# Sparse attention and a softplus layer on one core: another written-out order for the five engines

## The chip, the core and the metric

The kernel runs on one core of a Trainium2 chip. A core has five engines, each with an instruction queue of its own that it works off in order: TensorE (PE in the profile; PEld are its weight loads), VectorE (DVE), ScalarE (ACT), GpSimd (POOL) and SyncE (SP, which here only issues DMAs). Engines wait for one another through semaphores. The metric is the device time in microseconds (us).

## What is computed

For 4 batches of 8 heads, 768 positions and a head size of 64: keys are cut into chunks of 32; for each query the chunks are ranked by an upper bound of its scores (from each chunk's least and greatest key), and a causal softmax attention runs over the best six. Its output goes through a layer of 512 to 2048 to 512 with a softplus.

```python
k_min = np.min(k_chunks, axis=3)
k_max = np.max(k_chunks, axis=3)
ub = np.sum(np.maximum(q[:, :, :, None, :] * k_min[:, :, None, :, :], q[:, :, :, None, :] * k_max[:, :, None, :, :]), axis=-1)
...
top_chunks = np.argsort(ub, axis=-1)[..., -top_k:]
...
scores = np.where(mask, scores, -1000000000.0)
...
h = x @ w_in
g = np.maximum(h, 0.0) + np.log1p(np.exp(-np.abs(h)))
return (g @ w_out).astype(np.float32)
```

## The kernel before

The work is cut into 12 blocks of 256 queries, n = 0 to 11; three of them (k = n mod 3) make one batch. A block's heads are taken as four pairs. Every step of every block is an operation of a plan, made in `make_plan`; its name carries the block, as in kx3. These are the steps, in the order of a block's life:

- ld k, q, v (L378): loads from HBM with a cast to bf16, two for each tensor of a block, issued on GpSimd. Block 0's keys and queries come by SP and are cast on chip (cast).
- kD, qD (L499): transposition of keys and queries by a DMA, issued on SP, from block 3 on. Blocks 0 to 2 use TensorE instead (kT, qT, L495), with a copy (qc).
- kx, kn (L514, L522): greatest and least key of each chunk, on VectorE. bd (L298, into `bd`): these laid out as a block-diagonal operand. kc: the keys copied to their places (`ka`, `kb`).
- qpn (L571 on ScalarE, L573 and L575 on VectorE): positive and negative part of the queries. qac: the queries' copy for the other head of a pair.
- ub (L594): the chunk bounds, on TensorE; uba (L606), mx (L617, L621), raw (L636, L639): causal mask, the six greatest, and a raw 0/1 mask in `mraw`, on VectorE.
- mD (L660): the raw mask transposed by a DMA that SP issues (mT on TensorE before block 3). mc: the mask copied into spare rows of the query operand, so that the scores come out masked.
- s (L711, L712): scores on TensorE, into PSUM. ex (L719): exp on ScalarE. af (L729): the causal triangle set to zero on GpSimd. av (L741): products with the values. nm (L751, L752): division by the row sum, on VectorE.
- xD (L756): the result transposed by DMA, or oT (L767) on TensorE and a copy xc, for blocks 0, 1, 2 and 11.
- h (L910): product with w_in. e, ln (L915, L920): exp and ln(1 + e) on ScalarE, into `g`.
- y: product with w_out. Blocks 0, 1 and 11 do it plainly (L940). Blocks 2 to 10 use a scheme with seven products in place of eight (`seven`, L855), which needs differences of g (dl, dh, dd, de, df, L838) and combines the results (yr, yz, yv, yc, yd, ye, yw, yx, yf, L870). st (L952, L891): the store of 128 rows of output, issued on SP.
- ws, wd, wh, wv: for the seven products, rows of w_out are loaded once more (ws, L809, on SP, into the four `ysb` buffers that also hold outputs) and sums and differences of them are made (L815, on GpSimd or VectorE): wd and wh one half each (128 x 256), wv over the whole width (128 x 512). There are 8 wd, 16 wh and 8 wv. The first y of block 2 needs all the wv, its second product all the wh.

What stands where is not found at run time. A table, `ORDER` (L201 to L284), lists every operation once, and `in_order` reads it; an engine executes its operations in the table's order:

```python
for word in table.split():
    if word[0] == "z":
        order.append(int(word[1:]))
        continue
    name, _, which = word[1:].partition("#")
```

The letter in front of a name is the engine: P TensorE, A ScalarE, V VectorE, G GpSimd, S SP. A name stands for its next operation that has not been placed, or with # for a certain one. zN is N matrix products of zeros on TensorE, with no use but to keep it busy (L1025). Buffers and PSUM banks are given out in the table's order too, so an operation may also wait for the last reader of the buffer that it gets. Loads of the weights and of block 3 have fixed waits of their own (`gate`): block 3's loads wait for the last chunk of w_out.

Each engine's queue is strict: on GpSimd a load that stands behind an af waits until that af's exp is done; on SP a transposition that stands behind a ws waits until the buffer of this ws is free.

Of the kernel before, what the change touches and what calls it, by code (L numbers as in the profile page):

```python
# [213 lines left out]
Ps1 Ps2 Aex1 Ph0#5 Aex2 Gaf1 Gw_out2 PoT1 Pav1 Ae0#5 Pav1 Ps2#5 Ae0 Ps2#6 Vnm1 Gw_out3 Sws1.1 Sws1.0 Sws0.1 Sws0.0
Ph0 Aex2#5 Aex2#6 Gaf1 PoT1 Ps2#8 Gld_k4.0 Aln0 Pav1 Vxc1#2 Pav1 Vxc1 Ps2 Vnm1 Ph0 Gld_k4.1 Aex2 Aex2#8 PoT1 Ps2#3
Gld_k5.0 Ae0 Vxc1 Py0 Aex2#3 Gld_k5.1 Ps2 Ae0 Ps2 Vwh1 Ph1 Aex2 Vwv1 Gwh1 Aex2 Ps2#11 Gaf2#1 Ph0 Ae1 Gaf2 Aex2#11
Gld_q4.0 Pav2 Aln0 Pav2 Ps2#10 Gld_q4.1 Vnm2 Ps2 Ae0 Ph1 Vwd0 Aex2#10 Gaf2 Vwd1 Aln0 PoT2 Gaf2 Py0 Vwv0 Aex2 Ps2 Py0
Aex2 Ae1 Pav2 Ps2 Aln1 Pav2 Ps2#14 Ph1#4 Vnm2 Gld_k3.0 Aln0 Vwh0#1 Ph1 Gld_k3.1 Aex2 PoT2 Aex2#14 Ps2#16 SkD4
Gld_q3.0 Ae1 Py0 Axc2 Vxc2 Aex2#16 Ps2#18 Vye0 Sws2.0 Ae1#4 Ps2#20 Ph1 Aex2#18 Sws2.1 Aex2#20 Ph1#6 Ae1 Gaf2#6
Ps2#17 SqD4 Py0 Aex2#17 Aln1 Gaf2#5 Ps2#23 Ps2#15 Gld_q3.1 Py0 Aex2#15 Vkx4 SkD3 Aex2#23 Gld_q5.0 Ps2#19 Ph1#7  # L220
Aex2#19 Vkn4 Sohk Gld_q5.1 Ae1#6 Py0 Ae1#7 Gwh0 Vkc4 Ps2#22 Aln1#3 Ph1 Gwd2 Vwh2#1 Vbd4 Gaf2 Aex2#22 Ps2 Py0 Vkc4
Gaf2 Aex2 Gld_v3.0 Vqac4 Ps2 Aye0 Pav2 Gld_k6.0 Pav2 SqD3 Ae1 Py1 Vnm2 Aex2 Gwv2 Vkx3 PoT2 Pav2 Axc2 Pav2 Aln1 Gwh2
Py1 Sws3.0 Vnm2 Vkn3 Sohk PoT2 Py1 Axc2 Sws3.1 Ph2 Sst0 Vkc3 Aqpn3 SkD5 Vbd3 Ph2 Vqpn3 Ae2 Gwh3 Vqac3 Skb0 Pub3 Ae2
Gld_q10.0 Ph2 Vuba3 Vmx3 Ph2 Gld_v4.0 Vraw3 Py1 Gwv3 Sws4.1 Vqpn4 Aqpn4 Ae2 Aln2 Vwd3 Pub4 Ae2 Vkx5 Gwh3 Ph2#7
Sws4.0 Aln2 Gld_k6.1 SmD3 Vuba4 Ph2#6 Aye1 Vmx4 Gld_k9.0 Py1 Ae2#6 Gld_k9.1 Ae2#7 Ph2 Vraw4 Aln2#3 Gwh4#1 Vkn5 Ph2
# [834 lines left out]
```

## Time and profile before

| | us |
|---|---|
| median of 3 runs | 271.03 |
| lowest, highest | 269.88, 272.91 |
| profiled execution, its own time | 271.5 |
| its span, first to last instruction | 269.8 |
| TensorE busy | 254.3 |
| ScalarE busy | 220.6 |
| VectorE busy | 193.7 |
| GpSimd busy | 136.6 |
| mean granted TensorE clock | 0.987 of full |

All times in what follows count from the start of the span. The profile's row for a group of instructions gives its busy time, the mean of one in ns, the engine's idle time just before and what ended it. A row of the chain of waits gives start, length and what the end of the kernel was waiting for then; a row of the stretches gives, for a stretch of time, each engine's busy time with its count, then the granted clock, the DMA engines and GB/s.

### The profile page before, as it was taken

Reading aid. Unit: us, or ns where it says so; the run is one execution under the profiler, and the core shown is the slowest. Engines: PE = TensorE matmul, PEld = TensorE weight load, DVE = VectorE, ACT = ScalarE, POOL = GpSimd, SP = SyncE. Lnnn points to the kernel's source line nnn. Section 1 sums busy time; section 2 is a strip of 40 time slices with the busy share of each in tenths; the row PEclk is TensorE's granted clock in tenths of the full one; section 3 lists DMA queues with packets and bytes.
Section 4 is the critical chain, followed back from the end, with each engine's and each line's share of the span. In section 5 each row is a group of like instructions: output and inputs, shape, how many; then the busy total and the mean of one; then the engine's idle time right before and its main releaser. Section 6 shows DMA issues by size and latency. Waiting matters only on the chain.

```text
span 269.8 us, 7644 instructions
## 1 busy us (share of the span) xinstructions
PE 254.3 (94%) x2987; PEld 218.1 (81%) x2995; DVE 193.7 (72%) x589; ACT 220.6 (82%) x396; POOL 136.6 (51%) x220
## 2 busy tenths in 40 slices
PE   8899999995898779999999999999999999999995
PEld 7889898673575558889988899889899998899873
DVE  6788935449998998997989789887865526647310
ACT  3989899994587967899989999798989999756671
POOL 8986579467775967877675392330610411200000
PEclk9999999999799979999999999999999999999999
DMA  8999999999999999999999499654143040004004
GB/s 171 126 141 213 242 201 195 150 175 198 275 125 188 171 213 195 85 108 99 144 157 132 118 109 180 133 45 86 22 100 79 12 143 6 2 0 158 4 0 157
DMA packets 117028, 34.12 MB, mean 126 GB/s; under 512 B 104800, under 2 KB 111968, under 8 KB 116992
## 3 DMA queue, kind: packets, MB, share of 16 engines
q0 software_dynamic: 74944, 13.11, 63.8%
q1 hardware_dynamic: 42048, 20.52, 35.0%
q8 instruction: 23, 0.38, 0.6%
q14 instruction: 13, 0.11, 0.1%
HBM read 31.46 MB, written 6.29 MB: 140 GB/s over the span
## 4 chain that ended last, share of the span: by engine, by line
PE 62%; DVE 15%; DMA 10%; ACT 8%; issue 2%; SPq 1%; POOL 0%; ACTq 0%
PE ph L910 21%; PE py L855 9%; PE pt L855 9%; PE po L741 5%; PE ps L711 5%; PE ps L712 3%; DMA kT<-io 3%; DMA mT<-mraw 3%; ACT pt L719 2%; DVE kx L514 2%; DVE bd L298 2%; DMA qt<-io 2%; DMA wx<-in_q_dram 2%; PE py L940 2%; PE pt L711 1%
## 5 line engine op out<-in xcount | busy, mean ns | idle before, releaser
L910 PE MATMUL ph<-x,w_in_sb 128*128 128x256 bf16 x768 | 97.9, 275 | 0.2 <-ACT e L915 0.2
L719 ACT ACTIVATE pt<-ps 128x512 bf16<-128x512 f32 (+1 forms) x148 | 76.9, 551 | 9.4 <-PE ps L712 8.5
L910 PEld LDWEIGHTS <-w_in_sb 128*128 128x128 bf16 x768 | 73.7, 98 | 10.1 <-issue 0.7
L729 POOL TENSOR_SCALAR_AFFINE_SELECT pt<-pt 128x256 bf16<-128x256 bf16 x96 | 41.9, 459 | 70.1 <-ACT pt L719 63.9
L915 ACT ACTIVATE e<-ph 128x512 f32<-128x512 f32 x96 | 56.3, 600 | 13.7 <-PE ph L910 13.4
L920 ACT ACTIVATE g<-e 128x1024 bf16<-128x1024 f32 x48 | 50.5, 1060 | 0.6
L741 PEld LDWEIGHTS <-pt 128*128 128x128 bf16 x672 | 28.2, 99 | 4.3 <-POOL pt L729 1.9
L855 PEld LDWEIGHTS <-g 128*128 128x128 bf16 x288 | 27.3, 98 | 3.2
L741 PE MATMUL po<-v,pt 128*128 128x65 bf16 x538 | 25.6, 197 | 1.3 <-POOL pt L729 0.9
L719 ACT ACTIVATE pt<-pt 128x512 bf16<-128x512 f32 (+1 forms) x44 | 24.3, 557 | 1.6 <-PE pt L712 1.3
L514 DVE TENSOR_REDUCE kx<-kT 128x32 bf16<-128x1024 bf16 x18 | 21.5, 1210 | 3.6 <-DMA kT<-io 3.5
L855 PEld LDWEIGHTS <-df 128*128 128x128 bf16 x216 | 20.6, 97 | 2.8 <-issue 0.3
L378 POOL DMA_DIRECT2D v<-in_v_dram x24 | 21.8, 910 | 0.0
L711 PE MATMUL ps<-qt,kb 128*128 128x256 bf16 x75 | 20.3, 272 | 0.6 <-DVE qt L298 0.3
L1025 PE MATMUL py<-zero 128*128 128x128 bf16 x243 | 19.6, 234 | 1.1 <-DVE zero L307 1.1
L378 POOL DMA_DIRECT2D io<-in_k_dram x22 | 19.7, 909 | 1.3 <-DMA w_out_sb<-in_moe_w_out_dram 1.3
L711 PE MATMUL ps<-qa,ka 96*128 96x256 bf16 x73 | 19.5, 273 | 0.8 <-DVE qa L298 0.3
L940 PE MATMUL py<-w_out_sb,g 128*128 128x512 bf16 x72 | 19.6, 391 | 0.5 <-issue 0.2
L838 DVE TENSOR_TENSOR df<-g 128x1024 bf16<-128x1024 bf16 x27 | 18.7, 703 | 1.8 <-ACT g L920 1.0
L378 POOL DMA_DIRECT2D io<-in_q_dram x22 | 19.9, 906 | 0.1
L712 PE MATMUL ps<-qt,kb 128*128 128x128 bf16 (+1 forms) x75 | 18.3, 246 | 0.0
L752 DVE TENSOR_TENSOR osb<-po,rec 128x256 bf16<-128x256 f32 x39 | 16.6, 425 | 1.3
(132 smaller groups left out, 458.4 us busy)
## 6 DMA issues: line engine op xcount, KB each, us to landing
out_dram<-ysb SPq DMA_DIRECT2D x23, 256.0 KB, 2.3
ysb<-in_moe_w_out_dram SPq DMA_DIRECT2D x16, 256.0 KB, 4.9
v<-in_v_dram POOLq DMA_DIRECT2D x24, 128.0 KB, 5.2
io<-in_q_dram POOLq DMA_DIRECT2D x22, 128.0 KB, 5.0
io<-in_k_dram POOLq DMA_DIRECT2D x22, 128.0 KB, 5.3
w_in_sb<-in_moe_w_in_dram POOLq DMA_DIRECT2D x4, 512.0 KB, 9.3
w_out_sb<-in_moe_w_out_dram POOLq DMA_DIRECT2D x4, 512.0 KB, 10.8
wx<-in_k_dram SPq DMA_DIRECT2D x2, 256.0 KB, 3.2
```

The source lines that it names most:

```text
L378: lambda e, t=t: nc.gpsimd.dma_start(out=into(nm, n, t), in_=rows(nm, n, t)),
L514: nc.vector.tensor_reduce(kx.ap[:, :, j].rearrange("d p (t c) -> d t p c", t=NT), kT.ap.rearrange("d p x -> d (p x)").rearrange("d (t p c ...
L711: nc.tensor.matmul(sp.ap[:, 0:QB], kk[0:nr, p, j * 128:(j + 1) * 128], qq, start=True, stop=True)
L712: nc.tensor.matmul(sp.ap[:, QB:w], kk[0:nr, p, (j + 1) * 128:(j + 2) * 128], qq[:, 1] if last else qq, start=True, stop=True)
L719: lambda e, sp=sp, pt=pt, h=h, j=j, w=w: nc.scalar.activation(pt.ap[:, h, j:j + 2].rearrange("k j c -> k (j c)")[:, 0:w], sp.ap[:, 0:w], A ...
L729: nc.gpsimd.affine_select(out=d, in_=d, compare_op=ALU.is_ge, fill=0.0, base=0, channel_multiplier=-1, pattern=[[0, 2], [1, 128]])
L741: nc.tensor.matmul(o[:, u, h], pt.ap[:, h, j, c0:c0 + 128], T.V[i][:, j, 2 * p + h, :], start=(j == 0), stop=(j == t0 + u))
L855: nc.tensor.matmul(bank.ap[:, c * HD:(c + 1) * HD], a(f), w(f), start=start and f == 0, stop=f == HF - 1, skip_group_check=True)
L910: nc.tensor.matmul(o[:, j], T.w_in[:, dt, ft * 128:(ft + 1) * 128], x.ap[:, dt], start=(dt == 0), stop=(dt == KDM - 1))
L915: lambda e, hb=hb, eb=eb, f2=f2: nc.scalar.activation(eb.ap[:, f2 * 512:(f2 + 1) * 512], hb.ap, ACT.Exp),
L920: lambda e, eb=eb, g=g, f4=f4: nc.scalar.activation(g.ap[:, f4 * 4:(f4 + 1) * 4].rearrange("f j c -> f (j c)"), eb.ap, ACT.Ln, bias=1.0),
L940: nc.tensor.matmul(yb.ap[:, 0:c1 - c0], g.ap[:, f, u * 128:(u + 1) * 128], T.w_out[:, f, c0:c1], start=(f == 0), stop=(f == KFF - 1))
```

## The change

Only the table is replaced. The plan, its operations, the instruction that each of them issues, buffers and their sizes are the same; the operations stand in another order, and some run on another engine. Counted from the two tables:

- Weight sums: 19 of 32 stood on GpSimd, now 13. To VectorE go one wh2, both wh7, wv2, wv4, wv6, wd2, wd4 and wd7; to GpSimd go one wh0, wv0 and wd6.
- Output combinations (yw, yx): five go from GpSimd to VectorE, three the other way.
- Between ScalarE and VectorE: one mask copy of blocks 3 and 5 to ScalarE and one of block 9 to VectorE; query parts of blocks 0, 3, 8 and 11 to ScalarE, one of block 7 to VectorE; x copies of block 1 (one) and 11 (three) to ScalarE, of block 2 (two) to VectorE; and sixteen copies of y results, both ways.
- Products of zeros: 233 in place of 243.
- The order on all engines. Around block 3's mask, for example, the words were

```diff
-SmD4 Gld_v3.1 Ae2 Py1 Ae2 Vkc5 Gld_k7.0 Aln2 Py1 Vwh4 Gld_v4.1 Vkc3 Py1 Vmc3 Gwd4 SkD6 Vmc3 Gwv4 Ps3 Ps3#2 Aex3
...
+Vkx5 Aln2#3 SmD4 Gld_v4.0 Ph2 Ae2 Vwd4 Gld_q10.0 Sst0 Vwh4 Amc3#1 Py1 Vmc3 Gld_q6.0 Vkn5 Ps3 Ae2 Ps3#2 Py1 Aex3#2
```

and where the loads of blocks 3 to 5 begin

```diff
-Ph0 Aex2#5 Aex2#6 Gaf1 PoT1 Ps2#8 Gld_k4.0 Aln0 Pav1 Vxc1#2 Pav1 Vxc1 Ps2 Vnm1 Ph0 Gld_k4.1 Aex2 Aex2#8 PoT1 Ps2#3
...
+Ph0 Vxc1 Aex2 Ae0 Ps2#7 Gaf2 Py0 Ae0 Gw_out3 Sws1.1 Sws1.0 Sws0.0 Sws0.1 Aex2#7 Ph1 Gld_k5.0 Aln0#2 Vwd1 Vwv1 Ps2
+Gld_k4.0 Ph1 Aex2 Aln0 Gld_k4.1 Ps2#11 Pav2 Pav2 Ae1 Ps2 Gwh0 Vnm2 Py0 Ae1 Gld_q4.0 Vwh1 Aex2 Ph1 Vwd0 Aln0 Gaf2
```

GpSimd's own sequence there was: last two chunks of w_out, one af of block 1, k4.0, k4.1, k5.0, k5.1, a wh1, two af of block 2, q4.0, q4.1, two af, k3.0, k3.1, q3.0. It is now: all af of block 1, two af of block 2, last chunk of w_out, k5.0, k4.0, k4.1, a wh0, q4.0, an af, q4.1, q5.0, an af, k3.0, k3.1, wv0, a wh1, q3.0.

VectorE's sequence from the first reduction of block 4 to block 3's raw mask was: kx4 kn4 kc4 wh2 bd4 kc4 qac4 nm2 kx3 nm2 kn3 kc3 bd3 qpn3 qac3 uba3 mx3 raw3. It is now: kx4 kn4 kc4 kc4 wv2 wd2 wh2 wh2 qac4 nm2 kx3 xc2 nm2 kn3 bd4 bd3 kc3 kc3 qpn4 uba3 qac3 wd3 mx3 uba4 raw3.

SP's sequence up to that mask's transposition was: kD4, two ws2, qD4, kD3, a row copy, qD3, a ws3, a row copy, a ws3, st0, kD5, a row copy, two ws4, mD3. It is now: kD4, a ws2, qD4, a ws2, kD3, a ws3, qD3, kD5, a ws3, st0, three row copies, two ws4, mD3.

At the end, the store of the first half of block 8 stands between the last two stores of block 11, where before it stood among those of blocks 9 and 10.

More of the change, by code (lines that the diff above doesn't have):

```diff
@@ L284 @@
+Pav11 Ph10 Sst9 Vxc11#2 Vnm11 PoT11 Py10 Axc11 Py10 Ae10 PoT11 Py10 Axc11 Py10 Aln10 Ph11#2 Vde10 Ph11 Ae11#2 Vdh10
+Py10 Ae11 Vdd10 Py10 Vdf10 Ph11#6 Vyr10 Ph11 Ae11#6 Vyz10 Py10 Ae11 Py10 Aln11 Py10#12 Vyv10 Ph11 Py10 Ae11 Py10
+Aln11 Py10 Py10#13 Ph11#7 Ayd10 Vye10 Vyc10 Ph11#5 Vyw10 Ae11#7 Vyx10 Aln11#3 Py10 Sst10#1 Ph11 Vyf10 Sst10 Py11
+Ae11 Ae11 Py11 Aln11 Py11#4 Py11#8 Py11 Py11 Py11 Aye11 Py11 Py11 Sst11 Py11 Aye11 Py11 Sst11 Py11 Sst8 Aye11 Sst11
 """
```

160 lines of the change are left out of this document (78 added, 82 removed).

## The prediction

> **What bounds the kernel now.** I read the page first, then busy time by stretches of ten microseconds, then the chain of waits inside the bad stretches, and last the single instructions of the two engines named in it.
>
> ```profile
> PE 254.3 (94%) x2987; PEld 218.1 (81%) x2995; DVE 193.7 (72%) x589; ACT 220.6 (82%) x396; POOL 136.6 (51%) x220
> ...
> L1025 PE MATMUL py<-zero 128*128 128x128 bf16 x243 | 19.6, 234 | 1.1 <-DVE zero L307 1.1
> ```
>
> TensorE looks full at 94%, but 19.6 us of that are the matrix products of zeros with which the table fills idle stretches of the start. The stretches show where it is really full:
>
> ```profile
> 60.00:70.00 10.00, 6.66 (x71) 4.47 (x70) 9.37 (x12) 4.80 (x8) 6.61 (x10) 0.85 1.65 228
> 70.00:80.00 10.00, 9.10 (x93) 6.74 (x93) 9.79 (x38) 7.34 (x11) 9.55 (x11) 0.97 1.40 164
> ...
> 90.00:100.00 10.00, 7.10 (x101) 5.34 (x99) 9.75 (x26) 7.93 (x16) 7.86 (x15) 0.89 1.40 171
> ...
> 120.00:130.00 10.00, 10.00 (x145) 9.14 (x143) 8.57 (x31) 9.81 (x19) 8.36 (x14) 1.00 1.40 116
> ...
> 230.00:240.00 10.00, 10.00 (x113) 9.05 (x111) 4.95 (x10) 6.49 (x14) 1.48 (x4) 1.00 0.01 2
> ```
>
> The columns are TensorE, weight loads, VectorE, ScalarE and GpSimd, then the granted clock. From 120 us to the end TensorE has no hole: a new order can only lose there. Between 60 and 100 us it idles 3.3, 0.9 and 2.9 us in the rows shown, the clock falls to 0.85 and 0.89, and VectorE is the engine that is full (9.37, 9.79, 9.75). What it is busy with is the preparation of block 3:
>
> ```profile
> 50.17 7.28 DMA kT<-io
> ...
> 57.48 2.34 DVE kx L514 x2
> ...
> 76.10 0.20 DVE mraw L639
> ...
> 77.27 0.34 DVE wd L815
> ...
> 77.67 0.33 SPq L809
> ...
> 78.05 6.77 DMA mT<-mraw
> ...
> 85.19 0.27 PE ps L711
> ```
>
> So block 3's first scores (ps at 85.19) end a chain: keys of block 4 and 3 transposed by DMA, VectorE from 57.48 to 76.30 (when the raw mask is written), then 1.75 us in which the mask's transposition sits in SP's queue behind a weight load that waits for a weight sum (wd), then 6.77 us until it lands. In both tables the same TensorE work stands ahead of block 3's first h products; only the end of this chain can bring them forward. Inside it, VectorE is slow for one reason:
>
> ```profile
> 59.74 1.54 DVE L298 COPY ka<-kT 64x1024 bf16<-64x1024 bf16 x1
> 61.20 1.48 DVE L815 TENSOR_TENSOR wx<-ysb 128x256 bf16<-128x256 f32 x1
> 62.62 2.40 DVE L298 COPY bd<-kx 64x64 bf16<-64x64 bf16 x2
> 64.93 1.00 DVE L298 COPY kb<-kT 64x1024 bf16<-64x1024 bf16 x1
> ...
> 70.75 2.76 DVE L298 COPY bd<-kx 64x64 bf16<-64x64 bf16 x2
> ...
> 73.89 0.78 DVE L298 COPY qa<-qt 64x1024 bf16<-64x1024 bf16 x1
> ```
>
> ```profile
> 59.56 0.76 POOL L815 TENSOR_TENSOR wx<-ysb 128x256 bf16<-128x256 f32 x1
> ...
> 63.67 1.29 POOL L815 TENSOR_TENSOR wv<-ysb,ysb 128x512 bf16<-128x512 f32 x1
> ...
> 71.49 1.30 POOL L815 TENSOR_TENSOR wv<-ysb,ysb 128x512 bf16<-128x512 f32 x1
> 72.72 0.74 POOL L815 TENSOR_TENSOR wx<-ysb 128x256 bf16<-128x256 f32 x1
> 73.39 2.82 POOL L378 DMA_DIRECT2D io<-in_k_dram  x3
> ```
>
> ```profile
> L298 DVE COPY bd<-kx x26: 161/178/2086, 8.6 to 165.1; 64x64 bf16<-64x64 bf16 x22, 64x32 bf16<-64x32 bf16 x4
> L298 DVE COPY kb<-kT x9: 409/425/1002, 64.9 to 161.3; 64x1024 bf16<-64x1024 bf16 x9
> L815 DVE TENSOR_TENSOR wx<-ysb x6: 410/420/1484, 41.9 to 103.6; 128x256 bf16<-128x256 f32 x6
> L815 DVE TENSOR_TENSOR wv<-ysb,ysb x3: 682/884/1220, 42.2 to 93.8; 128x512 bf16<-128x512 f32 x3
> L815 DVE TENSOR_TENSOR wd<-ysb,ysb x4: 412/519/859, 46.3 to 108.4; 128x256 bf16<-128x256 f32 x4
> L514 DVE TENSOR_REDUCE kx<-kT x18: 1204/1209/1220, 57.5 to 156.6; 128x32 bf16<-128x1024 bf16 x18
> ```
>
> These are ns, least, median and greatest. A copy that takes 0.41 us takes 1.00 or 1.54 while GpSimd works; a pair of bd copies (2 x 0.16) takes 2.40 and 2.76. Over their least times the six rows hold 1.13 + 1.07 + 2.08 + 0.59 + 2.44 + 0.37 = 7.7 us (the same shape gives ka and qa their 0.41). The reductions never stretch.
>
> **The change, part by part.** The sum is made against the profiled execution, 269.8 us of span, 271.5 us in all, which is 0.5 us over the median; I take the difference to the median of 271.0.
>
> *Loads of block 4 and 3.* GpSimd's queue now has the last w_out chunk behind the second mask (af) of block 2, then k5.0, k4.0, k4.1.
>
> ```profile
> 37.71 1.51 POOL L413 DMA_DIRECT2D w_out_sb<-in_moe_w_out_dram  x2
> ...
> 39.57 3.54 POOL L378 DMA_DIRECT2D io<-in_k_dram  x4
> ...
> 43.96 0.76 POOL L729 TENSOR_SCALAR_AFFINE_SELECT pt<-pt 128x256 bf16<-128x256 bf16 x2
> ```
>
> ```profile
> DMA to landing us min/median/max: 3.8/5.2/9.6
> ```
>
> ```profile
> DMA to landing us min/median/max: 3.0/4.6/7.3
> ```
>
> These two masks end at 44.7 here, and what ScalarE has ahead of them differs by three short instructions. From there 0.76 for w_out and 2 x 0.89 for k5.0 and k4.0 put the issue of k4.1 at 47.3; the last two rows are issue to landing of the io loads and of the key transpositions. With 3.8 or 5.2 it lands at 51.1 to 52.5, against 50.17 when the transposition starts here. That one's 7.28 us are the greatest of nine; with a median 4.6 it ends 2.7 sooner, and one key load fewer (k5.1) is queued beside it. So the reduction kx4 starts between 1.7 us sooner and 2.4 later; I take +0.5, since nothing says which of the two ends holds.
>
> *VectorE's list from kx4 to the raw mask of block 3.* Against the old list it has in addition wv2 (0.68), wd2, wh2 and wd3 (3 x 0.41), a second kc3 copy (0.41), and two of some 0.35, an xc2 copy and block 4's uba: +3.0 us if nothing is held. Of 19 weight sums on GpSimd six net go to VectorE over the whole kernel.
>
> *Holds.* Between kx4 and this mask the old table has five sums on GpSimd, the new one three; loads and masks stay, and sixteen instead of eleven VectorE instructions (copies, and sums of two SBUF inputs) can be held. Bounds: none (-7.7) and all as now (0). After its loads GpSimd's next sum (wv3) has to wait for its weight rows, loaded behind block 5's transposition; meanwhile bd and kc of block 3 run free. I take 3.5 left, -4.2. On this the Trainium skill, page "SBUF — State Buffer", section "Who interferes with whom", says that the port pair shared by VectorE and GpSimd is locked for a whole instruction, and that a VectorE instruction with two SBUF inputs is blocked by a GpSimd one that reads SBUF. That speaks against the change, as a moved sum stays exposed; the trace agrees (1484 ns against 410), and with one blocking instruction per hold, as the rule has it, six more sums behind one mask each (0.76 for two above) would add at most 2.3 us. In the trace a single bd copy took 2086 ns, more than any one GpSimd instruction beside it, so the measurement goes beyond the rule.
>
> *SP's queue.* wd3 now stands ahead of block 3's maxima, so the weight load ahead of the mask's transposition finds its buffer free: -1.7 (bounds -1.75 and 0, if it waits for GpSimd's wv3 instead, which reads the same rows).
>
> *The mask's landing.*
>
> ```profile
> DMA to landing us min/median/max: 2.4/4.4/6.8
> ```
>
> This is mT's. 6.77 is the worst of nine. Fewer loads are issued just ahead of it: -0.5 (bounds -2.4 and 0).
>
> At ps the sum is 0.5 + 3.0 - 4.2 - 1.7 - 0.5 = -2.9.
>
> *From ps to y2.* One mask copy of block 3 goes to ScalarE, beside VectorE's: nothing. Two y1 steps, eight products of 512 columns, now stand behind ps instead of ahead of it.
>
> ```profile
> 263.20 1.73 PE py L940 x8
> ```
>
> Eight such take 1.7 us elsewhere in the chain; the 2.9 us hole of the 90 to 100 us row takes them: nothing, or their 1.7 if the hole were gone. The first y products of block 2 need all eight wv sums:
>
> ```profile
> L855 PE MATMUL py<-wv,g x72: 270/272/274, 107.3 to 247.0; 128*128 128x256 bf16 x72
> ```
>
> From the raw mask up to there VectorE gains wd4, wv4 and wv6 (0.41 + 2 x 0.68) and loses about as much (wh6, wd3, a kc3 and a mask copy); GpSimd loses seven, two of them moved up. But three wh sums and one wd are now left on VectorE for the time when y2 runs: +0.3, bounds -1.0 and +1.7.
>
> *The start and the end.* 233 filler products replace 243, ten of some 0.06 us that fill waits: nothing, and below nothing only if DMA came sooner. ScalarE takes three of the four last x copies, and a 256 KB store of block 8 is put ahead of the very last one.
>
> ```profile
> out_dram<-ysb SPq DMA_DIRECT2D x23, 256.0 KB, 2.3
> ```
>
> It costs between 0 and those 2.3; its issue falls into the last products, so I take +0.3.
>
> Together -2.9 + 0.3 + 0.3 = -2.3: 268.7 us.
>
> **Rivals.** *Holds gone.* If the exposed VectorE instructions fall between GpSimd's, holds are 1.0 or less, and if the mask lands in 4.4: another -2.5 - 1.9, of which I give 1.2 back, because y2 started at 107.3 with its sums and not with h3: 265.5. For it: six reductions and maxima cannot be held. Against: both engines' start times depend on loads that spread from 3.8 to 9.6.
>
> *VectorE longer and held as before (the other side).* Place: from kx4 to the raw mask. If GpSimd's loads sit back to back over kc4, qac4 and bd, as in 73.39, the holds stay near 7.7 while the list is 3.0 longer: 0.5 + 3.0 - 1.7 + 0.3 + 0.3 = +2.4, and with the late load +1.9 more: 273.4 to 275.3, say 274. It decides from holds of 5.8 us on, where the forecast's sum passes zero. For it: GpSimd is busy 9.55 of 10 us in the 70s, and queued loads are not fewer. Against: fewer sums, the longest holders.
>
> *It does nothing.* Block 3's queries land late (their load is now behind two sums), so ps is set by that transfer, and the rest is equal: 270.5 to 271.5.
>
> **How the numbers follow.** Forecast, 267.2 to 270.2: 0.40. Holds gone, 265.5: 0.25. Nothing: 0.15. Longer and held, 274: 0.20. With a quarter of the fast rival (0.06) and half of the slow one (0.10) left out the range is 265 to 274. One per cent, about what a measurement here can tell from no change, is 268.3 and 273.7: faster 0.25 and 0.13 of the forecast's 0.40, 0.38; slower 0.18 of the slow rival's 0.20; the rest, 0.44, within. The likeliest case by itself is 267.2 to 270.2.
>
> **What would show it.** Right: bd and kc copies near their least times between 57 and 76 us, the mask's transposition issued by 76 with no sum ahead of it on SP, ps by 82.5, the rows 60 to 80 nearer 9 for TensorE. Wrong: bd above 1 us again, kx4 after 60, SP's weight load ahead of the mask ended by GpSimd, or new TensorE holes after 110 us.

## The result and the profile after

The new order is slower: 279.46 us (278.43 to 280.63) against 270.95 us for the old one on the same chip, a ratio of 1.0307 with a 95% interval of 1.0229 to 1.0385. Its profiled execution took 280.3 us, with a span of 278.6. The ratios here compare only the runs within 1.5% of each kernel's fastest (for e13 two of six, for e5, e7 three of six), while medians and ranges are of all runs, so where runs scatter the two can differ.

The page of the new kernel, busy time by engine:

```profile
PE 254.7 (91%) x2979; PEld 217.5 (78%) x2985; DVE 187.8 (67%) x592; ACT 223.7 (80%) x401; POOL 126.5 (45%) x212
...
L1025 PE MATMUL py<-zero 128*128 128x128 bf16 x233 | 18.9, 232 | 1.1 <-DVE zero L307 1.1
```

VectorE is busy 5.9 us less than before although it has six more weight sums and two more output combinations, so it is held up less. GpSimd is busy 10.1 us less; part of that is the work that it gave away. TensorE does the same work in a span that is 8.8 us longer, so it waits more. Stretches of the new profile (TensorE, weight loads, VectorE, ScalarE, GpSimd, then the clock):

```profile
20.00:30.00 10.00, 8.35 (x156) 7.67 (x154) 8.56 (x37) 7.87 (x13) 8.55 (x17) 1.00 1.24 178
...
60.00:70.00 10.00, 8.85 (x96) 5.99 (x95) 9.63 (x21) 6.21 (x10) 6.85 (x10) 1.00 1.85 175
70.00:80.00 10.00, 6.00 (x65) 4.59 (x63) 3.81 (x24) 5.66 (x8) 3.88 (x4) 0.83 1.13 219
90.00:100.00 10.00, 7.51 (x84) 5.40 (x81) 9.77 (x16) 7.21 (x17) 7.91 (x17) 0.83 1.48 163
120.00:130.00 10.00, 10.00 (x116) 9.03 (x114) 9.08 (x32) 9.99 (x22) 6.66 (x10) 1.00 1.50 107
...
170.00:180.00 10.00, 7.96 (x87) 6.81 (x85) 7.16 (x26) 8.25 (x15) 4.74 (x9) 1.00 0.58 95
```

and the old profile in two stretches that the prediction did not show:

```profile
20.00:30.00 10.00, 9.59 (x182) 8.88 (x178) 8.98 (x46) 9.30 (x16) 6.08 (x14) 1.00 1.35 233
170.00:180.00 10.00, 10.00 (x105) 8.98 (x103) 8.43 (x28) 8.04 (x14) 3.84 (x7) 1.00 0.36 95
```

Three things are to be seen. The hole of the 60s has moved to the 70s, and there VectorE is no longer full but idle, at 3.81. The start has a hole that it did not have. And behind 120 us, where the old order had none, there are holes too.

To add this up, I take at four places the time at which a block's first product starts, less the TensorE work (without the zeros) that the table puts ahead of it, each step at its usual duration (0.872 us for an h step, 0.437 for a y step of the seven products, 0.22 for a full score step, and so on). What is left is TensorE time lost up to there; differences give the loss of each stage, in us, one profiled execution each (that of e11 is the longest of its six). A star marks a stage in the new order.

| | to first h of block 0 | to first scores of block 3 | to first h of block 4 | to first h of block 7 | to the end |
|---|---|---|---|---|---|
| old | 20.5 | 7.9 | 9.0 | 0.9 | 3.7 |
| new | 22.5* | 7.8* | 11.6* | 4.4* | 4.3* |
| new again (e9) | 24.2* | 7.1* | 11.2* | 3.4* | 3.5* |
| e4, old to h4 | 20.7 | 4.9 | 10.3 | 2.7* | 4.3* |
| e11, old to s3 | 21.1 | 5.5 | 12.1* | 6.9* | 3.8* |
| e15, old, mask first | 20.3 | 7.5 | 9.4 | 0.6 | 3.7 |

In the two profiles compared, the new order loses 2.0 us more than the old one in the start, no more up to block 3's scores, 2.6 more from there to block 4's h, 3.5 more from there to block 7's h and 0.6 more at the end. That the second stage shows no difference is in part chance. The old order lost 7.9 there in the execution that I read for the prediction and 7.5 in e15, but 4.9 and 5.5 in e4 and e11, which are the old order up to that point. That is where I looked for a gain. By block 4's h some of it is evened out: both stages together lose 16.9 in the old profile and in e15, and 15.2 in e4.

**The start.** GpSimd in the old profile, then in the new one:

```profile
18.39 0.42 POOL L314 TENSOR_SCALAR_AFFINE_SELECT ohb<-ohb 32x256 bf16<-32x256 bf16 x1
...
19.36 0.39 POOL L318 TENSOR_SCALAR_AFFINE_SELECT ohb<-ohb 32x256 bf16<-32x256 bf16 x1
19.71 2.19 POOL L729 TENSOR_SCALAR_AFFINE_SELECT pt<-pt 128x256 bf16<-128x256 bf16 x6
```

```profile
18.76 0.95 POOL L729 TENSOR_SCALAR_AFFINE_SELECT pt<-pt 128x256 bf16<-128x256 bf16 x2 [0.25 <-ACT pt L719]
...
20.94 1.12 POOL L729 TENSOR_SCALAR_AFFINE_SELECT pt<-pt 128x256 bf16<-128x256 bf16 x3 [0.51 <-ACT pt L719]
22.02 0.39 POOL L314 TENSOR_SCALAR_AFFINE_SELECT ohb<-ohb 32x256 bf16<-32x256 bf16 x1
```

The third ohb step has gone behind five masks of block 0, each of which waits for an exp. Two row copies on SP need it (`ohk`, 19.78 and 20.41 before, 23.36 and 23.99 now), and block 1's scores need the copies:

```profile
PE ps L711 <- DMA kb<-ohb: 2.4, 2, 1.3
```

This is from the new kernel's list of TensorE waits between 8 and 36 us (waited for, total, times, longest); the longer of the two, 1.3 us, is block 1's. The old profile has no wait for such a copy on TensorE's products.

**Block 3's queries.** ScalarE, TensorE and VectorE of the new kernel:

```profile
73.13 1.06 ACT L571 ACTIVATE qpos<-qt 128x1024 bf16<-128x1024 bf16 x1 [3.93 <-DMA qt<-io]
```

```profile
74.25 0.18 PE L594 MATMUL pt<-bd,qpos 128*128 128x16 bf16 x1 [3.24 <-ACT qpos L571]
```

```profile
59.13 2.34 DVE L514 TENSOR_REDUCE kx<-kT 128x32 bf16<-128x1024 bf16 x2 [3.83 <-DMA kT<-io]
61.48 0.88 DVE L298 COPY kb<-kT 64x1024 bf16<-64x1024 bf16 x1
62.38 0.87 DVE L298 COPY ka<-kT 64x1024 bf16<-64x1024 bf16 x1
...
69.09 0.73 DVE L298 COPY bd<-kx 64x64 bf16<-64x64 bf16 x4
...
75.84 0.57 DVE L573 TENSOR_SCALAR qneg<-qt 128x1024 bf16<-128x1024 bf16 x1 [5.13 <-PE pt L594]
```

The brackets give the idle time ahead and what ended it. The four bd copies, 2.40 and 2.76 us a pair in the old profile, take 0.73 together; nothing here is above 2.2 times its least time. Over their least times (0.41 for ka, kb and qa, 0.16 for a bd) kb, ka, bd and the two qa (0.47 and 0.62) hold 0.47 + 0.46 + 0.09 + 0.06 + 0.21 = 1.3 us, where the old six rows held 7.7. But then VectorE stands idle for 5.13 us, ScalarE for 3.93 and TensorE for 3.24, all for one transfer: the transposition of block 3's queries, which lands at 73.11 (68.35 in the old profile). All of what the shorter holds had won is waited away there.

That the holds went is no chance. All VectorE instructions from kx4 to the first mask copy of block 3, over the least time of their shape in any run, hold 2.5 us in the new profile and 9.9 in the old one. In the four other profiles that have the old order there (e1, e4, e11, e15) they hold 7.3 to 8.9, in the thirteen others with the new one 1.9 to 4.0. Among these is e8 (4.0), in which every weight sum has its old engine: the holds went with the order, and not with the engines of the sums.

Of the 4.8 us by which the query transposition lands later, 2.2 are its later issue (65.14 in place of 62.92) and 2.6 its longer way (7.98 us from issue to landing in place of 5.42). Which of the two would have been enough by itself was not tried.

**The mask copies.** Who waits for a mask's transposition (all blocks from 3 on), old and new, from the view of that tile:

```profile
  DMA mT<-mraw: 3.2, 3
```

```profile
  DMA mT<-mraw: 11.7, 8
...
  DVE qa L298: 7.9, 6
  ACT qt L297: 3.8, 2
```

In both orders the mask's copy into the queries stands on VectorE or ScalarE at a fixed place. In the new one the engine gets there earlier than the transposition lands, eight times for 11.7 us in all, and what is queued behind the copy, divisions of finished results among it, waits too.

From block 3's scores to the first y of block 2 another 2.9 us are lost: 85.39 to 110.4 now, 85.19 to 107.3 before. Of that, 1.7 us are the two y1 steps that now stand behind the scores. The first row below is from the new kernel's timeline of TensorE, the second from the view by tile of wv (times, then duration in ns, least, median and greatest, then first and last start).

```profile
85.39 0.27 PE L711 MATMUL ps<-qa,ka 96*128 96x256 bf16 x1
```

```profile
L855 PE MATMUL py<-wv,g x72: 269/272/274, 110.4 to 255.9; 128*128 128x256 bf16 x72
```

### The profile page after: what moved, and what is told of

It is laid out like the page before. It is cut to its first block, busy times and chain, and to the rows that moved or that the text cites. A ratio compares the mean times of both kernels' runs of the same rounds, so it can differ in the third digit from the quotient of the medians.

```text
span 278.6 us, 7610 instructions
## 1 busy us (share of the span) xinstructions
PE 254.7 (91%) x2979; PEld 217.5 (78%) x2985; DVE 187.8 (67%) x592; ACT 223.7 (80%) x401; POOL 126.5 (45%) x212
## 4 chain that ended last, share of the span: by engine, by line
PE 44%; DVE 11%; DMA 10%; ACT 4%; issue 2%; SPq 1%; DVEq 0%
PE ph L910 16%; PE py L855 8%; PE pt L855 6%; DMA mT<-mraw 6%; PE po L741 3%; PE ps L711 3%; DMA x<-osb 2%; PE ps L712 2%; DMA kT<-io 2%; DVE ub L621 2%; ACT pt L719 2%; DVE kx L514 2%; PE py L940 2%; DVE osb L752 1%; PE ph L940 1%
## 5 line engine op out<-in xcount | busy, mean ns | idle before, releaser
L719 ACT ACTIVATE pt<-ps 128x384 bf16<-128x384 f32 (+1 forms) x149 | 76.7, 549 | 10.6 <-PE ps L712 10.2
L910 PEld LDWEIGHTS <-w_in_sb 128*128 128x128 bf16 x768 | 73.6, 98 | 11.2 <-issue 1.2
L729 POOL TENSOR_SCALAR_AFFINE_SELECT pt<-pt 128x256 bf16<-128x256 bf16 x96 | 40.4, 439 | 86.3 <-ACT pt L719 79.6
L741 PEld LDWEIGHTS <-pt 128*128 128x128 bf16 x672 | 29.2, 99 | 5.2 <-issue 3.4
L711 PE MATMUL ps<-qt,kb 128*128 128x256 bf16 x75 | 19.5, 272 | 3.8 <-DMA kb<-ohb 2.4
L855 PEld LDWEIGHTS <-df 128*128 128x128 bf16 x216 | 20.5, 97 | 2.4
L1025 PE MATMUL py<-zero 128*128 128x128 bf16 x233 | 18.9, 232 | 1.1 <-DVE zero L307 1.1
L838 DVE TENSOR_TENSOR g<-g 128x1024 bf16<-128x1024 bf16 x18 | 12.9, 718 | 7.4 <-ACT g L920 7.2
L712 PE MATMUL ps<-qt,kb 128*128 128x256 bf16 (+1 forms) x75 | 17.8, 244 | 0.0
```

The lines of the kernel that those rows point to most:

```text
L711: nc.tensor.matmul(sp.ap[:, 0:QB], kk[0:nr, p, j * 128:(j + 1) * 128], qq, start=True, stop=True)
L719: lambda e, sp=sp, pt=pt, h=h, j=j, w=w: nc.scalar.activation(pt.ap[:, h, j:j + 2].rearrange("k j c -> k (j c)")[:, 0:w], sp.ap[:, 0:w], A ...
L729: nc.gpsimd.affine_select(out=d, in_=d, compare_op=ALU.is_ge, fill=0.0, base=0, channel_multiplier=-1, pattern=[[0, 2], [1, 128]])
L741: nc.tensor.matmul(o[:, u, h], pt.ap[:, h, j, c0:c0 + 128], T.V[i][:, j, 2 * p + h, :], start=(j == 0), stop=(j == t0 + u))
L838: return P.op(f"{nm}{n}", [("DVE", 640)], lambda e: nc.vector.tensor_tensor(out(), g.ap[:, a[0], a[1]], g.ap[:, b[0], b[1]], op=ALU.subtra ...
L855: nc.tensor.matmul(bank.ap[:, c * HD:(c + 1) * HD], a(f), w(f), start=start and f == 0, stop=f == HF - 1, skip_group_check=True)
```

## The experiments

Where two orders are joined, the first stands up to the named product, and then follows what is left, in the order of the other. Time is the median and range of all runs, and the difference to the old order's median on the same chip.

**Where along the order is the loss?** Two theories first: *piecewise*, each stretch of the new order has a loss of its own; and *absorbed* or *echo*, one place is late and the rest follows from it, or takes it up.

```diff
-new order throughout
+new order up to Ph0 (e1), Ps3 (e2), Ph3 (e3), the rest in the old order
+old order up to Ph4 (e4), the rest in the new order
```

> The new table up to block 0's first h product (31.8 us in its profile, 29.6 in the old one), then everything that is left in the old table's order. Theory 'piecewise' (each stretch of the new table has a loss of its own, and they add up to the 8.5 us): the start is 2.2 us late and stays late, about 273.2 us. Theory 'absorbed' (block 3's preparation ends at a time that loads and VectorE set, so a late start is taken up by the old table's TensorE holes at 64 to 67 and 90 to 98 us): 270.8 to 271.5 us.

273.28 us (270.28 to 275.76), +1.8; ratio 1.0044 (0.9999 to 1.0088). Between the two; the interval just reaches no difference.

> The new table up to block 3's first score product (85.2 us in both profiles), then the old order. Piecewise: the profiles show 2.3 to 2.7 us more idle TensorE time by then, so 273.4 us. Absorbed: since this product starts at the same 85.2 us in both, at most 272 us. My prediction's view (this stretch is where the change gains 2.9 us): 268.5 us.

276.07 us (275.32 to 276.62), +4.6; ratio 1.0174 (1.0098 to 1.0249). By the medians the stretch in which I had forecast the gain costs some 3 us.

> The new table up to block 3's first h product (102.7 us in its profile, 98.7 in the old one), then the old order. Piecewise: 4.0 us late there, of which the old table's later holes (0.5 us up to 120) can take little: 274.5 us. If the loss is only one of the tail behind 110 us: 271 to 272 us.

277.69 us (275.68 to 279.37), +6.2; ratio 1.0213 (1.0103 to 1.0323). More than piecewise asked, though the interval, of four runs, covers e2 too.

> The old table up to block 4's first h product (117 us), then the new order. Piecewise: what the new profile loses behind that point, 8.8 minus 4.6, so 275 us. My prediction's view (TensorE has no hole there, the tail costs 0.3): 271.3 us. If the tail's holes in the new profile are only the echo of a late beginning (buffers and loads out of step): 271 to 272 us.

273.22 us (271.13 to 274.79), +1.8; ratio 1.0068 (1.0024 to 1.0112). The tail of the new order costs something even after an old beginning; the prediction had it free. It is less than half of the 4.2 us that piecewise asked for, so part of the tail's loss is an echo. The profiles of e2 and e3 say the same: from block 4's h to block 7's they run the old order and lose 2.3 and 2.5 us, where the old kernel loses 0.9.

Most of the loss is in pieces, by the medians with the largest, 2.8 us, between block 0's h and block 3's scores; some of what is lost in the tail echoes the beginning. The complement, run later, agrees:

```diff
-new order throughout
+old order up to Ps3, the rest in the new order
```

> The old table up to block 3's first score product, then the new order. By the lost TensorE time of the profiles so far the new order loses 4.7 us more than the old one up to that point and 4 to 5 behind it. Piecewise: 274.5 to 276 us. Echo: 271 to 273 us.

274.7 us (273.26 to 278.95), +4.2; ratio 1.0137 (1.0097 to 1.0177). As piecewise said.

**Single places of the new order, mended.** On GpSimd, block 3's query loads (e5); the third ohb (e6); on VectorE, what is held between 90 and 101 us (e7); the old engine for each weight sum (e8):

```diff
-Gld_k3.1 Gwv0 Gwh1 Gld_q3.0 Gaf2 Gwh0 Gld_q3.1
+Gld_k3.1 Gld_q3.0 Gld_q3.1 Gwv0 Gwh1 Gaf2 Gwh0
```

> The new table, but on GpSimd block 3's two query loads (q3.0, q3.1) stand right behind its key loads, as in the old table, instead of behind one wv sum, two wh sums and a mask. In the new profile q3.1 is issued at 58.27 and lands at 65.05, its transposition lands at 73.11 (68.35 in the old one), and ScalarE, VectorE and TensorE all wait until then: TensorE 3.2 us from 71.0. Theory 'queries late' (this wait is the main part of the 3.5 us that the stretch up to block 3's scores costs): the load goes out about 3 us sooner, TensorE's wait falls below 1 us, 276 to 277.5 us in place of 279.5. Theory 'VectorE' (its list from the reduction of block 4 to the raw mask is what is long; it is idle from 70.7 to 75.8 only by chance): 279 us or more.

280.02 us (276.0 to 281.58), +9.2; ratio 1.0237 (1.017 to 1.0305). In its profile TensorE's wait of 3.2 us for `qpos` is gone and the stage up to block 3's scores loses 5.4 in place of 7.8, but the kernel is not faster beyond the scatter. The rest of that profile, of the longest of the six runs, is worse: the start loses 25.2, and the stage from h4 to h7 7.9. The reason for the latter is the best example of the mask copies. VectorE, then TensorE's waits:

```profile
143.17 0.68 DVE L837 TENSOR_TENSOR df<-g 128x1024 bf16<-128x1024 bf16 x1
147.51 0.58 DVE L297 COPY qa<-mT 32x512 bf16<-32x512 bf16 x2 [3.65 <-DMA mT<-mraw]
148.11 0.36 DVE L297 COPY bd<-kx 64x64 bf16<-64x64 bf16 x2
148.50 0.18 DVE L750 RECIPROCAL rec<-po 128x4 f32<-128x4 f32 x1
148.72 0.42 DVE L751 TENSOR_TENSOR osb<-po,rec 128x256 bf16<-128x256 f32 x1
```

```profile
PE po L740 <- DVE osb L751: 2.7, 1, 2.7
```

VectorE does nothing for 3.65 us because the mask copy of block 7 is next in its queue and the mask has not landed; two places behind it stands the division of block 6 whose PSUM bank TensorE needs. The Trainium skill, page "Perfetto Trace Analysis", section "Tensor Engine Instruction (MATMUL, LD_WEIGHTS)", says that ScalarE, VectorE and GpSimd are strictly first in, first out; this row agrees, with 3.65 us.

```diff
-Gld_v1.0 Gaf0 Gaf0 Gw_in1 Gaf0 Gaf0 Gaf0 Goh
+Gld_v1.0 Goh Gaf0 Gaf0 Gw_in1 Gaf0 Gaf0 Gaf0
```

> The new table, but the third ohb operation on GpSimd (three instructions, 1.3 us) stands ahead of the five masks of block 0 that it was put behind, as in the old table. In the new profile it ends at 23.3, so block 1's two row copies go out at 23.4 and 24.0 (19.8 and 20.4 in the old one) and TensorE waits for the second until 29.1. Theory 'row copies' (that is the whole loss of the start): block 0's first h product 1.5 to 2 us sooner than 31.8, 278 us. Theory 'other causes at the start' (ScalarE's order): h at 31 or later, 279 us or more.

281.27 us (279.48 to 284.29), +10.4; ratio 1.0347 (1.0294 to 1.04). TensorE's wait for block 1's row copies is gone from the profile, but the first h came at 32.4, so the theory that this is the whole loss of the start falls. In this execution, the longest of the six, TensorE waited for a second row copy of block 0, 1.2 us; and the new start holds 42 products of zeros in one piece (2.51 us here and in the new profile), which TensorE works off whether the wait is there or not. How much of the start either makes was not separated; from here on the old start is taken as a whole.

```diff
-Vnm3 Vbd5 Vdh2 Vnm3 Vkx6 Vnm3 Vkn6 Vnm3 Vwh5 Vwv5 Vqpn5 Vnm4 Vbd6 Vuba5
+Vnm3 Vdh2 Vnm3 Vbd5 Vkx6 Vnm3 Vkn6 Vnm3 Vqpn5 Vnm4 Vbd6 Vuba5 Vwh5 Vwv5
```

> The new table, but VectorE's bd of block 5 stands behind the second division of block 3, and the weight sums wh5 and wv5 behind block 5's causal mask. In the new profile this bd is held for 1.87 us beside a run of six masks on GpSimd and wh5 for 2.80 us beside four masks and two sums, and TensorE waits 1.4 us at 93.3 and 0.45 at 101.3 for what stands behind them. Theory 'holds' (the GpSimd wait that the change was to remove came back here): 1.5 to 2.5 us less, 277 to 278 us. Theory 'no matter' (the stretch from 85 to 110 is set by ScalarE's exps and the transpositions on SP): 279 to 280 us.

282.4 us (278.83 to 284.73), +11.6; ratio 1.0332 (1.027 to 1.0394). It is no faster, but it does not decide between the theories, since only one of the two holds went. The new kernel's VectorE, then its GpSimd, with the two holds:

```profile
91.17 2.23 DVE L298 COPY bd<-kx 64x64 bf16<-64x64 bf16 x2
...
97.94 2.79 DVE L815 TENSOR_TENSOR wx<-ysb 128x256 bf16<-128x256 f32 x1
```

```profile
91.16 2.20 POOL L729 TENSOR_SCALAR_AFFINE_SELECT pt<-pt 128x256 bf16<-128x256 bf16 x6
...
97.58 1.13 POOL L729 TENSOR_SCALAR_AFFINE_SELECT pt<-pt 128x256 bf16<-128x256 bf16 x3
98.67 0.72 POOL L815 TENSOR_TENSOR wd<-ysb,ysb 128x256 bf16<-128x256 f32 x1
99.36 0.40 POOL L729 TENSOR_SCALAR_AFFINE_SELECT pt<-pt 128x256 bf16<-128x256 bf16 x1
99.73 0.71 POOL L815 TENSOR_TENSOR wx<-ysb 128x256 bf16<-128x256 f32 x1
```

In e7 wh5 is free (0.43 us), but beside the same run of six masks the difference dh, which now stands where bd stood, is held instead: 2.37 us in place of 0.69. VectorE and GpSimd of e7:

```profile
91.83 2.37 DVE L837 TENSOR_TENSOR df<-g 128x1024 bf16<-128x1024 bf16 x1
```

```profile
91.82 2.65 POOL L728 TENSOR_SCALAR_AFFINE_SELECT pt<-pt 128x256 bf16<-128x256 bf16 x6
```

```diff
-Vwv2 Vwd2 Vwh2 Vwd4 Vwh4 Vwv4 Vwv6 Vwh7 Vwh7 Vwd7 Gwv0 Gwh0 Gwh4 Gwd6
+Gwv2 Gwd2 Gwh2 Gwd4 Gwh4 Gwv4 Gwv6 Gwh7 Gwh7 Gwd7 Vwv0 Vwh0 Vwh4 Vwd6
```

> The new table's order with the old table's engine for each of the 14 weight sums that changed it (ten back to GpSimd, four back to VectorE). If the choice of engine is what costs: 271 to 274 us. If it helps, as my prediction had it (holds 4.2 us less against 3.0 us more on VectorE): 281 us or more, with bd held above 1 us again between 57 and 80 us. If it is the order: 278 to 280 us.

281.93 us (276.98 to 286.4), +11.1; the scatter leaves no ratio, but even the fastest of the six is 3.9 us over the slowest of the old order on that chip (273.12). The old engines of the weight sums do not bring the time back, so their choice does not make the loss; nor did bd go above 1 us between 57 and 80 us. What is left is the order, with the other engine changes.

**Mends together.** The kernels e9, e10 and e12 ran on one chip with e11. The mask copies (e10) were moved back by two to four instructions of their engine, with a score product (Ps9) where it has to follow:

```diff
-Amc5 Vmc5 Vwh7 Vwh6 Ps5
+Vwh7 Amc5 Vwh6 Vmc5 Ps5
...
-Vmc7 Vbd10 Vnm6 Vkc9 Ps7
+Vbd10 Vnm6 Vkc9 Vmc7 Ps7
...
-Vmc9 Vdd5 Vqac8 Ps9 Vkc11 Vnm7 Ps9
+Vdd5 Vqac8 Vkc11 Vnm7 Vmc9 Ps9 Ps9
```

> The new table unchanged, as the measure for the next three on the same chip: 279 to 282 us. Both theories expect idle time of VectorE and ScalarE in front of the mask copies of blocks 3 to 11 of 12 us or more (12.8 in the new profile, 3.6 in the old one).

278.18 us (275.88 to 285.45), +7.7; ratio 1.0255 (1.0205 to 1.0304). In its profile the mask copies wait 11.3 us in seven places, a little less than expected.

> The new table with six mask copies moved back by two to four instructions on their engine (mc5, mc6, mc7, mc9 on VectorE, mc5 and mc6 on ScalarE), so that other work is done while the mask's transposition lands. Theory 'landings' (in the new order the engines stand at the head of their queues and wait for transpositions, and TensorE waits for what is queued behind): 2 to 4 us faster than the unchanged new table, nearly all of it between block 5's and block 7's first h product. Theory 'echo' (the tail only loses because it begins late and out of step): within 1 us of it.

275.52 us (272.62 to 281.12), +5.0; ratio 1.0168 (1.0121 to 1.0214): 2.7 us less than the unchanged new table. The wait for masks goes as 'landings' said, and the loss from h4 to h7 goes from 3.4 to 1.9. That stage varies, though: e17, e12 and e16, which have the later copies too, lose 2.3, 3.5 and 3.8 us in it, the ten profiles with the new order there and without them 2.7 to 8.6. The mask waits of e10:

```profile
  DMA mT<-mraw: 2.4, 4
```

> The new table with the old order up to block 0's first h product, block 3's query loads ahead of the sums on GpSimd, and the six mask copies later, all three at once. If these three places hold the loss: 271 to 273.5 us. If the loss is spread over the whole order and they only show where it was read first: 276 us or more.

272.24 us (271.31 to 276.38), +1.7; ratio 1.0066 (1.0034 to 1.0098). Three places hold some 6 of the 7.7 us by the medians, 5 by the ratios.

Which holds what: the old start alone, the start with the query loads, and the two pairs that were missing? The first edit below is in e13, e14 and e16, the second in e14 and e17, and e10's mask copies in e16 and e17:

```diff
-new order up to Ph0
+old order up to Ph0
...
-Gwv0 Gwh1 Gld_q3.0 Gaf2 Gwh0 Gld_q3.1
+Gld_q3.0 Gld_q3.1 Gwv0 Gwh1 Gaf2 Gwh0
```

> The old order up to block 0's first h product, then the new order, with nothing else mended. If the start by itself holds its 2 to 3 us to the end: 275 to 277 us (new table 278 to 279.5). If a start on time is lost again in the wait for block 3's queries: 278 us or more.

279.22 us (272.47 to 280.55), +9.4; ratio 1.0145 (1.0056 to 1.0233). The median is on the side of 'lost again', but two of the six runs, 272.47 and 276.49, are not, so this run decides little. In its profile, of one of the long runs (280.14), TensorE still waits 3.1 us for block 3's `qpos`.

> The same with block 3's query loads ahead of the sums on GpSimd, so that it differs from the fully mended one (272.2 us) only by the six mask copies. If the mask copies hold 2 to 3 us here too, 274.5 to 275.5 us; if the query loads hold nothing, the same as the run with the old start alone.

274.7 us (272.94 to 277.79), +4.9; ratio 1.0184 (1.0127 to 1.0241). The mask copies hold their 3 us here too.

> The old start and the six mask copies later, the query loads as in the new table. With all three mended the kernel is 1.7 us over the old one; with the start and the query loads mended 4.9; with the start alone 9.4; with the masks alone 5.0; with the query loads alone 9.2. If the mask copies are worth 2.5 to 3 us whatever else is mended and the query loads 4: about 6 us over the old one. If the three only work together: 7 us or more.

275.39 us (273.71 to 277.36), +5.2; ratio 1.0192 (1.0145 to 1.024). Nearer to the first.

> The query loads early and the six mask copies later, the new start kept. If the start is worth its 2 to 3 us at the end once the other two are mended: 4 to 5 us over the old table. If the start is absorbed behind: 2 to 3 us over it. If the query loads are worth nothing without the old start: 5 us or more, as with the masks alone.

275.23 us (273.6 to 281.44), +5.0; ratio 1.0171 (1.0128 to 1.0215). The same as with the masks alone.

| mended | us over the old order, medians | ratio | block 3's query transposition lands at |
|---|---|---|---|
| nothing (e9; the new kernel) | 7.7; 8.5 | 1.0255; 1.0307 | 73.8; 73.1 |
| start (e13) | 9.4 | 1.0145 | 71.6 |
| query loads (e5) | 9.2 | 1.0237 | 72.7 |
| masks (e10) | 5.0 | 1.0168 | 72.5 |
| start and query loads (e14) | 4.9 | 1.0184 | 68.4 |
| start and masks (e16) | 5.2 | 1.0192 | 72.1 |
| query loads and masks (e17) | 5.0 | 1.0171 | 71.0 |
| all three (e12) | 1.7 | 1.0066 | 68.2 |

By the medians the mask copies are worth 3 to 4 us whatever else is mended (7.7 to 5.0, 9.4 to 5.2, 9.2 to 5.0, 4.9 to 1.7), and the start and the query loads 3 us together and nothing alone. The last column suggests why: with a late start the masks and exps ahead of the loads on GpSimd are late too, and the loads with them; with the loads behind the sums an early start only waits longer. Only with both does the transposition land at 68.2 or 68.4, as in the old profile (68.35). Block 3's first scores follow: they start at 80.91 in e14 and 81.49 in e12, but at 84.66 in e13 and 84.63 in e16, which differ from those two in the query loads alone. That is the cost of the late queries, 3.1 to 3.8 us there. Yet up to these scores e14 and e12 lose 4.9 and 5.9 us by the measure of the table of losses, no less than the old order in e4 and e11 (4.9 and 5.5): even with the queries on time the new order gains nothing on those.

Six runs of a kernel scatter over 4 to 10 us, so the first steps of this table are not firm: the intervals of the single mends overlap that of the unmended kernel, and by the ratios start to start and masks is no gain at all. Firm are the two ends, 1.0255 (1.0205 to 1.0304) unmended and 1.0066 (1.0034 to 1.0098) with all three, and each last step: with two of the three mended the ratio is 1.0171 to 1.0192, and none of those intervals reaches that of all three. So, by the ratios, each of the three is worth some 3 us once the other two are mended.

**The prediction's own term.** In the old table, the mask's transposition ahead of the two weight loads on SP, and nothing else:

```diff
-Sws4.1 Sws4.0 SmD3
+SmD3 Sws4.1 Sws4.0
```

> The old table with one change: on SP the transposition of block 3's mask stands ahead of the two weight loads ws4 instead of behind them. My prediction put 1.7 us on this at block 3's scores (the mask is written at 76.30 and its transposition issued at 78.05 in the old profile). If that term reaches the end: 269 to 269.5 us. If something else sets those scores or the time is lost again at the first y of block 2: 270 to 271 us.

271.24 us (269.07 to 274.11), +1.4; ratio 1.003 (0.9993 to 1.0068). No gain. Its VectorE and SP show what the prediction overlooked:

```profile
72.41 0.57 DVE L638 CAST mraw<-ub 128x16 bf16<-128x16 f32 x1
72.87 1.53 DVE L574 TENSOR_SCALAR qpos<-qt 128x1024 bf16<-128x1024 bf16 x1
...
76.78 1.36 DVE L620 MAX8 ub<-pt 128x8 f32<-128x12 f32 x16
...
81.02 1.75 DVE L814 TENSOR_TENSOR wx<-ysb 128x256 bf16<-128x256 f32 x1
82.78 1.39 DVE L297 COPY kb<-kT 64x1024 bf16<-64x1024 bf16 x1
84.20 0.60 DVE L297 COPY qa<-mT 32x512 bf16<-32x512 bf16 x2
```

```profile
73.01 1.21 SPq L659 DMA_TRANSPOSE mT<-mraw  x1
```

```profile
84.54 0.27 PE L710 MATMUL ps<-qa,ka 96*128 96x256 bf16 x1 [2.55 <-DVE qa L297]
```

The raw mask is written at 72.98, the transposition goes out at 73.01, 5 us sooner than in the old profile, and lands at 77.72, 7.1 us sooner. Its copy still starts at 84.20 (84.85 before) and the scores at 84.54 (85.19): between raw3 and that copy VectorE has a query part, a weight sum, a reduction, block 4's causal mask, its sixteen maxima, its raw mask, another reduction, two copies and a weight sum to do. In this execution 4.1 us of holds fall on that list (the weight sum of 1.75 and the copy of 1.39 above are two of them), where the old profile has 0.8; without them the scores could have started sooner, so this profile alone does not settle the term. The twelve runs do as to the time at the end. With the old order at this place (the old profile, e1, e4, e11) VectorE waited for the mask at that copy for 1.10, 0.45, 0 and 1.09 us: the mask was never more than 1.1 us from being on time.

No version tried beats the old order.

## Why the prediction was wrong

It was 268.7 us, with a range to 274; measured were 279.46. Two steps of it failed: the gain of 2.9 us at block 3's first scores, in whose place block 3's queries came late, and the tail behind block 4's h, which was said to have only losses to give and got no term. Step by step:

- **What bounds the kernel: half right.** The lost time of the old profile was read where it is, and the chain through it was real in that execution. But "only the end of this chain can bring them forward" took it for the only chain. In e15 most holds between kx4 and raw3 are gone (the bd pairs take 1.06 and 0.36 us), the mask lands 7 us sooner, and the scores start 0.65 us sooner. VectorE's own list up to the mask copy, with the holds that now fall behind raw3, is as long as the chain that I followed.
- **Start of kx4, +0.5 within -1.7 to +2.4: held.** 59.13 in place of 57.48, +1.65.
- **VectorE's list, +3.0: beside the point.** It was not the bound: VectorE is idle 5.13 us in it.
- **Holds, -4.2 with 3.5 left: right, and too small.** 1.3 are left of 7.7 by the rows above. The rival on the other side needed 5.8 or more and is out. The reason that I gave, fewer sums on GpSimd, is not needed for it: with the old engines (e8) the holds are nearly as short, 4.0 us by the sum over all instructions, against 2.5 in the new kernel and 7.3 to 9.9 with the old order.
- **SP's queue, -1.7: the order is as read** (the transposition goes out at 80.05, right behind the raw mask), **the worth is not**: e15.
- **The mask's landing, -0.5 within -2.4 to 0: outside, on the good side.** 3.03 us in place of 6.77.
- **Sum at ps, -2.9: a step that failed.** The scores start at 85.39, and two y1 steps fewer are done by then, so it is 0.2 + 1.7 later. What took the place of the holds is the transposition of block 3's queries, which lands at 73.11 with VectorE idle for 5.13 us. With the query loads early, and nothing else changed, the scores start 3.1 to 3.8 us sooner (e14 against e13, e12 against e16). It was named, as the mechanism of the rival "it does nothing" ("their load is now behind two sums"), but with "the rest is equal" for a price and a chance of 0.15. I had costed the new GpSimd sequence only as far as block 4's keys; carried on, the same durations (a wv 1.29, a wh 0.75, a mask 0.4, a load 0.9) would have put block 3's queries behind everything.
- **From ps to y2, +0.3 within -1.0 to +1.7: outside.** It is 2.9 worse. The 1.7 that I set at nothing because a later hole would take it are in that; what the rest is was not found. The stage between s3 and h4 loses 9.0 to 12.1 in the rows above, in either order. Whether the returned holds (1.87 and 2.79 us) make part of it stays open, since e7 moved one of them to another instruction.
- **The start, "nothing": wrong by some 3 us.** Over all profiles, up to the first h, the eight with the old start lose 20.3 to 21.1 (median 20.65), the eleven with the new one 21.8 to 25.2 (median 23.4). I counted the zeros there and did not look at what GpSimd does between them.
- **The tail: "a new order can only lose there", and then no term for it; the other step that failed.** From h4 to h7 it loses 2.7 to 6.9 in the rows above where the old order loses 0.6 to 0.9, 3.5 us between the two profiles compared, the largest single piece. Part of it is an echo of the late beginning (e2 and e3); moving the mask copies, for which VectorE and ScalarE waited 11.7 us, takes 2.7 us off the kernel by the medians (e10). The signs that would show the prediction wrong had "new TensorE holes after 110 us", with no price on them.
- **The end, +0.3: right as to size.** Both orders lose 3.5 to 4.3 in the last stretch.

What stays open: which part of the start costs what, how the start and the query loads share their 3 us, what the stage from s3 to h4 loses its time to, and the last 1.7 us of the mended kernel.

## What to carry to other kernels

When an order of all engines is replaced, what is full in the old profile has no gain to give but a loss to take, so it needs a term too: go through the whole list of each in-order queue for instructions that wait for a transfer, and see how much other work stands between the transfer's issue and that instruction. An exposed wait that is taken away is worth only the distance to the next queue that is late, and that distance is measured by making the one thing early and nothing else, as e15 did. And a chain that is read in one execution should be checked against a second one before it is called the bound.

## What the runs showed of the hardware

- A VectorE instruction can be held through a whole run of GpSimd instructions, not for one: a bd copy of 0.16 us took 1.87 beside six back-to-back masks of 2.20 us together, and a weight sum of 0.41 us took 2.79 beside four masks and two sums. The Trainium skill, page "SBUF — State Buffer", section "Who interferes with whom", which the prediction drew on, says that whoever issues first gets the shared port pair for the whole instruction. Read as one blocking instruction per hold, as the prediction read it, that is too little: each mask is some 0.4 us and each of the two sums 0.7, and these holds are longer than any one of them.
- Which instruction is held varies between executions, and how much is held in all goes with the order. With the old order of VectorE and GpSimd from kx4 to raw3 the two bd pairs took 2.40 and 2.76 us in one execution (old), 2.23 and 0.36 in another (e4) and 1.06 and 0.36 in a third (e15), but up to the mask copy the sum of all holds was 9.9, 8.6 and 7.3 us. With the new order it was 1.9 to 4.0 in fourteen executions.
- The transposition of a mask lands after anything from 2.4 to 6.5 us in one execution (new profile), one of queries after 3.0 to 8.0, without any change in size. For that of block 3's queries the nineteen profiles show what the long ones go with: it took 4.3 to 5.4 us when three to six other transfers were under way at its issue, and 6.4 to 8.0 when there were seven or eight. No run here takes transfers away and nothing else, to show that they are the cause.
